# Scoring two groups and summing two pieces in one visit of TensorE, in a fused attention and squared-ReLU MLP loop

## The chip, the cores and the metric

The kernel runs on one NeuronCore of a Trainium2 chip. The metric is the device time of one execution in microseconds (us). The engines are named as in the profile: PE (TensorE matmul), PEld (its weight loads), DVE (VectorE), ACT (ScalarE), POOL (GpSimd) and SP (SyncE, whose queue issues the DMAs). Each works through its own instructions strictly in the order in which they were written, and waits on semaphores for the others.

## The reference

```python
B, N, C = (4, 12480, 128); n_agents = 49; d_ff = 2048
scale = 1.0 / np.sqrt(q.shape[-1])
def sm(a, b):
    s = scale * (a @ b.transpose(0, 2, 1))
    s = s - s.max(-1, keepdims=True)
    e = np.exp(s)
    return e / (e.sum(-1, keepdims=True) + 1e-09)
agent_v = sm(agents, k) @ v
x = (sm(q, agents) @ agent_v).reshape(B * N, C)
h = x @ w_in
r = np.maximum(h, 0.0)
return (r * r) @ w_out
```

Per batch, 49 agents attend to 12480 keys and gather `agent_v`; then each of the 12480 queries attends to the 49 agents, and its result goes through an MLP of width 2048 with a squared ReLU. All is float32.

## The kernel before

**Tiling.** Tokens come in groups of 960 (8 chunks of 120): 13 groups per batch and 52 in all. Query groups are numbered s = 0 to 51, the pieces of keys and values n = 0 to 12 in their batch b. The attention output is never formed: `w_make` multiplies `agent_v` into `w_in` once per batch (`w_hi`, `w_lo`), and the loop multiplies the query probabilities (`p_a`, and `p_b`, the same with its two halves of partitions exchanged by two DMAs, `q_spread`) by that product.

**The main loop** has 832 steps i, 16 per query group. Step i does `mm1` on PE (six matmuls into a tile `h`; there are two `h` buffers), `relu` on ACT (`h` to `rg`), and at odd steps, for the two steps together, `square` on ACT, `high` on DVE (`gh`, a rounded copy of `rg`) and `low` on DVE (`gl`, the remainder). About five steps later `mm2` (twelve matmuls) multiplies `gh` and `gl` by `wo_hi` and `wo_lo` and adds into a pair of PSUM banks. There are two such pairs. Eight steps make one output tile of 480 tokens in one pair; then `store` empties it (ACT and DVE, then a DMA), and the pairs change places.

**Visits.** The attention work of later groups is woven into the loop. Its matmuls go on PE between two steps and write into the pair that `mm2` is not using (`bank()`); here this is called a visit. Before there are these visits, for each group or piece: `k_scores` (keys times agents, 16 float32 matmuls of 49 columns), `q_scores` (the same for queries), `q_transpose` and `v_acc` (16 matmuls of 258 columns). Each is followed by a reader of the bank: `k_copy` (ACT), `q_shift` (DVE: `q_max` and `q_sub`), `q_copy` (ACT) and `v_sum` (DVE, adds into `acc`). Behind `q_shift` come `q_exp` on ACT, `q_inverse` on DVE, `q_norm` on POOL, `q_hi` on ACT, `q_lo` on POOL, then `q_transpose`. For keys and values: `k_pmax` on DVE, later `k_sub` (POOL), `k_exp` and `k_hi` (ACT), `k_lo` (POOL), `v_hi` (ACT) and `v_lo` (DVE), then `v_acc`. Batch 0's keys and values are done ahead of the loop; those of batches 1, 2 and 3 during the groups of the batch before.

**What sets the order.** A planner, `chain`, puts each part at a step number t, and all parts are written out sorted by t. A visit stands at t = g + .45, and g must be a step in `slots`: three of the eight steps of an output tile. ACT and DVE get at most one such part per step (`taken`) at + .5. In a step: `mm1` at + 0, `relu` at + .1, `mm2` and `store` at + .2, `square` at + .55, `high` at + .6, `low` at + .65. A DVE part that reads a bank right behind a visit stands at + .47 of the visit's step, and the `low` of the pair of steps before is then set to + .48 (`read`), that is, behind it. Loads are put some steps ahead of their use (`k_load`, `q_load`, `v_load`); they share five buffers (tag `io`) in the order in which they are written, and SP issues all DMAs from one queue.

Of the kernel before, what the change touches and what calls it, by code (L numbers as in the profile page):

```python
# [9 lines left out]
F32 = mybir.dt.float32  # L10
# [15 lines left out]
def agent_attention_relu2_kernel(ctx: ExitStack, tc: tile.TileContext, qT, kT, v, agT, w_in, w_out, outT):  # L26
# [14 lines left out]
    A2 = 2 * A  # L41
# [3 lines left out]
    rc = (slice(0, L), slice(L, CH))  # L45
# [10 lines left out]
    ag_sb = cpool.tile([P, B, A], F32, name="ag_sb")  # L56
# [69 lines left out]
    sk = cpool.tile([CH, NCH, A], F32, name="sk")  # L126
    pm = cpool.tile([CH, NS, A], F32, name="pm")
# [10 lines left out]
    H = G // 2  # L138
    halves = (slice(0, H), slice(H, G))

    kts, vts, pes, pss, two = {}, {}, {}, {}, [None]
# [5 lines left out]
    def bank():  # L147
        if now[0] is None:
            return ps_h.tile([P, 2, 512], F32, name="h")
        return pairs[now[0]]  # L150
# [4 lines left out]
    def piece(n):  # L155
        return sk[:, n * G:(n + 1) * G, :]
# [2 lines left out]
        kts[b, n] = (wk if b + n // 4 == 0 else io).tile([P, G, CH], F32, name="kt", tag="io" if b + n // 4 else turned[n])  # L159
        nc.sync.dma_start(out=kts[b, n], in_=kT[b, n])  # L160

    def scores(ps, x, b, cs=range(G)):
        for c in cs:
            for r in rc:
                nc.tensor.matmul(ps[r, 0, c * A:(c + 1) * A], x[:, c, r], ag_sb[:, b, :], start=True, stop=True)  # L165
        return ps[:CH, 0, :G * A].rearrange("p (c a) -> p c a", a=A)

    def k_scores(b, n):
        pss["k", n] = scores(bank(), kts.pop((b, n)), b)

    def k_copy(n):
        nc.scalar.copy(piece(n), pss.pop(("k", n)))

    def k_pmax(n):
        nc.vector.tensor_reduce(out=pm[:, n, :], in_=piece(n).rearrange("p c a -> p a c"), axis=AX.X, op=ALU.max)

    def k_pmax_bank(n):
        nc.vector.tensor_reduce(out=pm[:, n, :], in_=pss["k", n].rearrange("p c a -> p a c"), axis=AX.X, op=ALU.max)  # L178

    def k_max(step):  # L180
        if step == 0:
# [37 lines left out]
    vss = []  # L219
# [10 lines left out]
        vs = vss[n % 2][:, halves[h]]  # L230
        eng.tensor_tensor(out=vs[:, :, C + 2:], in0=vts[n][:, halves[h], :C], in1=vs[:, :, :C].bitcast(F32), op=ALU.subtract)

    def v_acc(n):
        vs, pe = vss[n % 2], pes.pop(n)
        vts.pop(n)
        pss["v", n] = bank()
        for c in range(G):
            for u in range(2):
                nc.tensor.matmul(pss["v", n][:A2, u, :VW], pe[rc[u], c, :], vs[rc[u], c], start=c == 0, stop=c == G - 1)  # L239

    def v_acc_whole(n, ps):

# [50 lines left out]
        else:  # L293
            nc.vector.tensor_tensor(wl[:, js], pss.pop(("w", b, j)), wh[:, js].bitcast(F32), op=ALU.subtract)

    PT, qs, es, mxs, sms, pps = {}, {}, {}, {}, {}, {}

    def q_load(s):
        qs[s] = (io if s else wk).tile([P, G, CH], F32, name="qt", tag="io" if s else "p_b")
        nc.sync.dma_start(out=qs[s], in_=qT[s])  # L300

    def q_scores(s):
        pss["q", s] = scores(bank(), qs.pop(s), s // NS)

    def q_scores_part(s, x):
        if x == 0:
            pss["q", s] = bank()
            scores(pss["q", s], qs[s], s // NS, range(H))
        else:
            pss["q", s] = scores(pss["q", s], qs.pop(s), s // NS, range(H, G))  # L310

    def q_max(s):
        mxs[s] = wk.tile([CH, G, 1], F32, name="mx")
        nc.vector.tensor_reduce(out=mxs[s], in_=pss["q", s], axis=AX.X, op=ALU.max)

    def q_sub(s):
        es[s] = wk.tile([CH, G, A], F32, name="e")
        nc.vector.tensor_tensor(es[s], pss.pop(("q", s)), mxs.pop(s).to_broadcast([CH, G, A]), op=ALU.subtract)

    def q_shift(s):  # L320
        q_max(s)
        q_sub(s)

    def q_exp(s):
        nc.scalar.activation(es[s], es[s], AF.Exp, scale=scale)
# [94 lines left out]


    LAG = 5
    AHEAD = 0
    steps = []

    def at(t, f, *args):
        steps.append((t, len(steps), f, args))
# [3 lines left out]
    hop = {"PE": {"PE": 1, "ACT": 1, "DVE": 0}, "ACT": {"PE": 2, "ACT": 1, "DVE": 0, "POOL": 0, "SP": 0},  # L431
           "DVE": {"PE": 2, "ACT": 1, "DVE": 1, "POOL": 1, "SP": 0}, "POOL": {"PE": 3, "ACT": 2, "DVE": 2, "POOL": 1}}
# [6 lines left out]
    def chain(t, todo):  # L439

        first = prev = None
        while todo:
            n = 1
            while todo[0][0] == "PE" and n < len(todo) and todo[n][1] in reads_bank and todo[n][0] != "PE":
                n += 1
            t += hop[prev][todo[0][0]] if prev else 0
            while True:
                g, p, ts = t, None, []  # L450
                for e, *_ in todo[:n]:
                    g += hop[p][e] if p else 0
                    while (e, g) in taken or (e == "PE" and g not in slots):
                        if p == "PE" and e == "DVE":
                            break
                        g += 1
                    ts.append(g)
                    p = e
                if todo[0][0] != "PE" or ts[-1] <= ts[0] + 1:
                    break  # L460
                t += 1
            for (e, f, *args), g in zip(todo, ts):
                soon = e == "DVE" and prev == "PE"
                if soon:
                    read.add(g)
                else:
                    taken.add((e, g))
                at(g + (.47 if soon else .45 if e == "PE" else .5), f, *args)
                prev = e
            first = ts[0] if first is None else first  # L470
            t, todo = ts[-1], todo[n:]
        return first, t

    reads_bank = (k_copy, k_max, v_sum, a_final, w_make, q_shift, q_copy)

    def plan_tokens(s, base):
        todo = [("PE", q_scores, s), ("DVE", q_shift, s), ("ACT", q_exp, s), ("DVE", q_inverse, s),
                ("POOL", q_norm, s), ("ACT", q_hi, s), ("POOL", q_lo, s),
                ("PE", q_transpose, s), ("ACT", q_copy, s)]
        first, end = chain(base, todo if s > 1 else todo[2:])  # L480
        if s > 1:
            at(first - 6, q_load, s)
        at(end + .9, q_spread, s)
        assert end + 3 < s * NF, (s, end)

    def plan_batch(b, base):

        end = b * NS * NF
        for n in range(NS):
            if b == 1 and n < AHEAD:  # L490
                continue
            first, t = chain(base + int(n * 4.6), [("PE", k_scores, b, n), ("ACT", k_copy, n), ("DVE", k_pmax, n)])
            if b > 1 or n:
                at(max(base - (6 if b > 1 else 0), first - 8), k_load, b, n)
            if n == NS - 2:
                chain(t + 1, [("DVE", k_max, 0)])
        _, t0 = chain(t + 1, [("DVE", k_max, 1), ("PE", k_max, 2), ("DVE", k_max, 3), ("PE", k_max, 4), ("DVE", k_max, 5)])
        free = {}
        d = (end - 37 - t0) / NS
        for n in range(NS):  # L500
            t, r = t0 + 1 + int(n * d), free.get(n - 2, 0) + 1
            first, _ = chain(max(t - 2, r), [("ACT", v_hi, n, 0), ("DVE", v_lo, n, 0)])
            _, t2 = chain(max(t - 1, r), [("ACT", v_hi, n, 1), ("DVE", v_lo, n, 1)])
            at(first - 6, v_load, b, n)
            _, t1 = chain(max(t, r - 3), [("POOL", k_sub, n), ("ACT", k_exp, n), ("ACT", k_hi, n), ("POOL", k_lo, n)])
            _, t = chain(max(t1 + 3, t2 + 2), [("PE", v_acc, n), ("DVE", v_sum, n)])
            free[n] = t - 1
        _, e = chain(t + 1, [("DVE", a_final, 0, b), ("PE", a_final, 1, b), ("DVE", a_final, 2, b)])
        for j in range(0, NJ, 4):
            _, e = chain(e + 2, [("PE", w_make, b, j // 4, j, 4, 0), ("ACT", w_make, b, j // 4, j, 4, 1), ("DVE", w_make, b, j // 4, j, 4, 2)])  # L510
        assert e + 2 < end, (e, end)
        return t + 1
# [28 lines left out]
    for n in range(NS):  # L541
        t = Z + 6.3 + 2.07 * n
        at(t, use, None if n % 3 else 1)
        at(t, k_scores, 0, n)
        at(t + .1, warm_up, 5 if n < NS - 1 else 0)
        at(t + 1.5, k_pmax_bank, n)
        at(t + 1.51, k_copy, n)
# [8 lines left out]
    at(t0 - 1.1, k_max, 0)  # L556
    at(t0 - .24, use, None)
    at(t0 - .23, q_scores_part, 0, 0)
    at(t0 - .1, use, 1)
    at(t0 - .05, warm_up, 2)  # L560
    for x, y in zip(range(1, 6), (-.1, 0, .5, .6, 2.6)):
        at(t0 + y, k_max, x)
    at(t0 + .3, warm_up, 2)
    at(t0 + .65, q_scores_part, 0, 1)
    at(t0 + .66, warm_up, 2)
    t0 += 2
# [18 lines left out]
    t = t0 + 15.9  # L585
# [72 lines left out]
```

## Time and profile before

| | |
|---|---|
| median of 3 runs | 1908.52 us (1907.07 to 1908.65) |
| the profiled execution | 1906.95 us |
| its span, first to last instruction | 1905.2 us |
| TensorE clock granted | 0.999 |
| PE busy | 1892.5 us (99%) |
| DVE busy | 1750.9 us (92%) |
| ACT busy | 1721.8 us (90%) |
| POOL busy | 355.3 us (19%) |

A group's row in the profile has the line, the engine, the operation, the tiles written and read, the count, the busy time, the mean duration of one in ns, and the idle time of the engine before it with what ended it. Records of one instruction overlap by about a tenth of a microsecond with the next on ACT and DVE, so the pitch is shorter than the duration. A row of the timeline has start and duration in us. The first step of the loop starts at 55.4 us.

### The profile page before, as it was taken

Reading aid. Unit: us, or ns where it says so; the run is one execution under the profiler, and the core shown is the slowest. Engines: PE = TensorE matmul, PEld = TensorE weight load, DVE = VectorE, ACT = ScalarE, POOL = GpSimd, SP = SyncE. Lnnn points to the kernel's source line nnn. Section 1 sums busy time; section 2 is a strip of 40 time slices with the busy share of each in tenths; the row PEclk is TensorE's granted clock in tenths of the full one; section 3 lists DMA queues with packets and bytes.
Section 4 is the critical chain, followed back from the end, with each engine's and each line's share of the span. In section 5 each row is a group of like instructions: output and inputs, shape, how many; then the busy total and the mean of one; then the engine's idle time right before and its main releaser. Section 6 shows DMA issues by size and latency. Waiting matters only on the chain.

```text
span 1905.2 us, 45852 instructions
## 1 busy us (share of the span) xinstructions
PE 1892.5 (99%) x20204; PEld 1669.1 (88%) x20204; DVE 1750.9 (92%) x1476; ACT 1721.8 (90%) x1809; POOL 355.3 (19%) x199
## 2 busy tenths in 40 slices
PE   9999999999999999999999999999999999999998
PEld 8788889988888998898888898998988888888888
DVE  7888999999889999999888999999989898989987
ACT  5788999998888999999888999999989999999997
POOL 0110233231012223324001223224201010000100
PEclk9999999999999999999999999999999999999999
DMA  9322222311331221211232121221211111111110
GB/s 369 107 71 82 83 63 62 92 42 51 104 98 41 81 63 53 75 57 57 79 97 62 57 75 52 66 79 41 64 36 35 50 33 53 36 36 53 35 38 22
DMA packets 44760, 130.95 MB, mean 69 GB/s; under 512 B 5034, under 2 KB 18474, under 8 KB 44562
## 3 DMA queue, kind: packets, MB, share of 16 engines
q1 hardware_dynamic: 44562, 128.04, 21.7%
q8 instruction: 158, 2.59, 0.6%
q14 instruction: 40, 0.33, 0.1%
HBM read 82.89 MB, written 25.56 MB: 57 GB/s over the span
## 4 chain that ended last, share of the span: by engine, by line
PE 96%; DVE 2%; DMA 1%; ACT 1%; issue 0%; SPq 0%; DVEq 0%
PE pair L412 57%; PE h L384 29%; PE pair L165 5%; PE pair L239 2%; PE pair L352 2%; DMA raw<-w_in 1%; DVE gl L401 0%; PE pair L290 0%; DMA kt<-kT 0%; DMA vt<-v 0%; DVE sk L197 0%; ACT rg L393 0%; DVE pm L178 0%; DVE cv L100 0%; DVE gh L397 0%; DVE cv L101 0%
## 5 line engine op out<-in xcount | busy, mean ns | idle before, releaser
L401 DVE TENSOR_TENSOR gl<-rg,gh 128x1920 fp32r<-128x1920 f32 x416 | 947.9, 2279 | 14.9 <-DVE gh L397 0.9
L390 ACT ACTIVATE rg<-h 128x960 f32<-128x960 f32 x832 | 804.5, 974 | 139.7 <-PE h L384 139.1
L393 ACT ACTIVATE rg<-rg 128x1920 f32<-128x1920 f32 x416 | 756.4, 1818 | 5.9
L412 PE MATMUL pair<-gh,wo_lo 64*128 64x480 f32 x3328 | 655.8, 378 | 0.0
L412 PE MATMUL pair<-gh,wo_hi 64*128 64x480 f32 x3328 | 654.7, 378 | 0.4 <-DVE gh L397 0.4
L397 DVE CAST gh<-rg 128x1920 fp32r<-128x1920 f32 x416 | 503.3, 1210 | 95.7 <-ACT rg L393 88.6
L384 PE MATMUL h<-p_a,w_hi 49*128 49x480 f32 x1664 | 511.8, 386 | 0.6 <-ACT rg L390 0.6
L412 PE MATMUL pair<-gl,wo_hi 64*128 64x480 f32 x3328 | 509.7, 376 | 1.8 <-DVE gl L401 1.8
L384 PE MATMUL h<-p_b,w_hi 49*128 49x480 f32 x1664 | 507.6, 385 | 0.0
L412 PEld LDWEIGHTS pair<-gh,wo_lo 64*128 64x128 f32 x3328 | 339.1, 186 | 36.3
L412 PEld LDWEIGHTS pair<-gh,wo_hi 64*128 64x128 f32 x3328 | 336.5, 184 | 37.6 <-DVE gh L397 0.8
L412 PEld LDWEIGHTS pair<-gl,wo_hi 64*128 64x128 f32 x3328 | 329.7, 184 | 44.0 <-DVE gl L401 4.2
L384 PEld LDWEIGHTS h<-p_a,w_hi 49*128 49x128 f32 x1664 | 291.1, 185 | 27.2 <-issue 2.4
L384 PE MATMUL h<-p_a,w_lo 49*128 49x480 f32 x832 | 311.1, 374 | 0.0
L384 PE MATMUL h<-p_b,w_lo 49*128 49x480 f32 x832 | 311.1, 374 | 0.0
L384 PEld LDWEIGHTS h<-p_b,w_hi 49*128 49x128 f32 x1664 | 293.1, 185 | 13.6
L337 POOL TENSOR_TENSOR e<-e,sm 120x392 f32<-120x392 f32 x51 | 80.7, 1582 | 1023.5 <-DVE sm L334 865.7
L384 PEld LDWEIGHTS h<-p_a,w_lo 49*128 49x128 f32 x832 | 152.6, 183 | 17.9
L384 PEld LDWEIGHTS h<-p_b,w_lo 49*128 49x128 f32 x832 | 152.7, 184 | 0.7
L344 POOL TENSOR_TENSOR pp<-e,pp 120x392 fp32r<-120x392 f32 x51 | 96.8, 1898 | 150.3 <-ACT pp L341 150.3
L207 POOL TENSOR_TENSOR pe<-sk,pe 120x392 fp32r<-120x392 f32 x39 | 76.5, 1962 | 253.3 <-ACT pe L204 253.3
L197 POOL TENSOR_TENSOR sk<-sk,mM 120x392 f32<-120x392 f32 x39 | 97.0, 2488 | 0.0
(112 smaller groups left out, 1170.9 us busy)
## 6 DMA issues: line engine op xcount, KB each, us to landing
vt<-v SPq DMA_DIRECT2D x52, 516.0 KB
kt<-kT SPq DMA_DIRECT2D x52, 480.0 KB
qt<-qT SPq DMA_DIRECT2D x52, 480.0 KB
outT<-ob SPq DMA_DIRECT2D x104, 240.0 KB
p_b<-p_a SPq DMA_DIRECT2D x104, 183.8 KB
raw<-w_in SPq DMA_DIRECT2D x4, 512.0 KB
raw<-w_out SPq DMA_DIRECT2D x4, 512.0 KB
ag_sb<-agT SPq DMA_DIRECT2D x1, 98.0 KB
```

What stands on the lines that cost most here:

```text
L165: nc.tensor.matmul(ps[r, 0, c * A:(c + 1) * A], x[:, c, r], ag_sb[:, b, :], start=True, stop=True)
L197: eng.tensor_tensor(out=piece(n), in0=piece(n), in1=m.rearrange("p (o a) -> p o a", o=1).to_broadcast([CH, G, A]), op=ALU.subtract)
L207: eng.tensor_tensor(out=pes[n][:, :, A:], in0=piece(n), in1=pes[n][:, :, :A].bitcast(F32), op=ALU.subtract)
L239: nc.tensor.matmul(pss["v", n][:A2, u, :VW], pe[rc[u], c, :], vs[rc[u], c], start=c == 0, stop=c == G - 1)
L337: eng.tensor_tensor(out=es[s], in0=es[s], in1=sms.pop(s).to_broadcast([CH, G, A]), op=ALU.mult)
L344: eng.tensor_tensor(out=pps[s][:, :, L:], in0=es.pop(s), in1=pps[s][:, :, :A].bitcast(F32), op=ALU.subtract)
L384: nc.tensor.matmul(h[:, u, :TT], w[ra[u], j, :], PT[s][u ^ lo][ra[u], cs, :], start=x == 0, stop=x == 2)
L390: nc.scalar.activation(rgs[p][:, x], hs.pop(i)[:, :, :TT], AF.Relu)
L393: nc.scalar.activation(rgs[p], rgs[p], AF.Square)
L397: nc.vector.tensor_copy(ghs[p], rgs[p])
L401: nc.vector.tensor_tensor(out=gls[p], in0=rgs.pop(p), in1=ghs[p].bitcast(F32), op=ALU.subtract)
L412: nc.tensor.matmul(outs[t][u][:, :TT], w[rg[u], 2 * j + e, :], g[rg[u], e, :], start=j == 0 and x == 0, stop=j == NJ - 1 and x == 5)
```

## The change

Scores of two groups go into the two banks of one pair in one visit, and one instruction reads both: `k_copy` for two key pieces, the two instructions of `q_shift` for query groups s and s + 1 (s even, from 2). `v_acc` accumulates two pieces in one visit, and `v_sum` adds them together. All other parts remain one for each group or piece. `k_copy` moves from the step behind the visit to the visit's own step, at + .47 (`ACTs`). `q_shift` moves from + .47 to + .49, behind `low`; `v_sum` stays at + .47. The exponentials, sums and transposes of the odd groups come some 15 steps behind those of the even ones. The two buffers of the shifted scores become one tile `eb`. Two loads of a pair are written at the same place.

```diff
-    def k_scores(b, n):
-        pss["k", n] = scores(bank(), kts.pop((b, n)), b)
-
-    def k_copy(n):
-        nc.scalar.copy(piece(n), pss.pop(("k", n)))
+    def both(ps, n):
+        return ps[:CH, :n, :G * A].rearrange("p u (c a) -> p u c a", a=A)
+
+    def k_scores(b, n, m=1):
+        ps = bank()
+        for u in range(m):
+            scores(ps, kts.pop((b, n + u)), b, u)
+        pss["k", n] = both(ps, m)
+
+    def k_copy(n, m=1):
+        nc.scalar.copy(sk[:, n * G:(n + m) * G, :].rearrange("p (u c) a -> p u c a", u=m), pss.pop(("k", n)))
...
+    def v_acc(n, m):
+        ps = pss["v", n] = bank()
+        for x in range(n, n + m):
+            vs, pe = vss[x % 2], pes.pop(x)
+            vts.pop(x)
+            for c in range(G):
+                for u in range(2):
+                    nc.tensor.matmul(ps[:A2, u, :VW], pe[rc[u], c, :], vs[rc[u], c], start=x == n and c == 0, stop=x == n + m - 1 and c == G - 1)
...
-    def q_scores(s):
-        pss["q", s] = scores(bank(), qs.pop(s), s // NS)
+    def q_scores(s, m=1):
+        ps = bank()
+        for u in range(m):
+            scores(ps, qs.pop(s + u), (s + u) // NS, u)
+        pss["q", s] = both(ps, m)
...
+    def q_shift(s, m=1):
+        mx = wk.tile([CH, 2, G, 1], F32, name="mx")[:, :m]
+        for x in range(s, s + m):
+            es[x] = eb[:, x % 2]
+        nc.vector.tensor_reduce(out=mx.rearrange("p u c o -> p u (c o)"), in_=pss["q", s], axis=AX.X, op=ALU.max)
+        nc.vector.tensor_tensor(eb[:, s % 2:s % 2 + m], pss.pop(("q", s)), mx.to_broadcast([CH, m, G, A]), op=ALU.subtract)
...
-                soon = e == "DVE" and prev == "PE"
-                if soon:
+                soon = e in ("DVE", "ACTs") and prev == "PE"
+                if soon and e == "ACTs":
+                    e = "ACT"
+                elif soon:
                     read.add(g)
                 else:
                     taken.add((e, g))
-                at(g + (.47 if soon else .45 if e == "PE" else .5), f, *args)
+                at(g + (.49 if soon and f is q_shift else .47 if soon else .45 if e == "PE" else .5), f, *args)
...
-        first, end = chain(base, todo if s > 1 else todo[2:])
-        if s > 1:
-            at(first - 6, q_load, s)
+        if s > 1 and s % 2 == 0:
+            first, base = chain(base, [("PE", q_scores, s, 2), ("DVE", q_shift, s, 2)])
+            for x in (s, s + 1):
+                at(first - 6, q_load, x)
+            base += 1
+        _, end = chain(base, todo)
...
+        for n in range(0, NS, 2):
+            m = min(2, NS - n)
+            first, t = chain(base + int(n * 4.6), [("PE", k_scores, b, n, m), ("ACTs", k_copy, n, m)])
+            for x in range(n, n + m):
+                _, t = chain(t + 1, [("DVE", k_pmax, x)])
+                if b > 1 or x:
+                    at(max(base - (6 if b > 1 else 0), first - 8), k_load, b, x)
...
+            if n % 2 or n == NS - 1:
+                x = n - n % 2
+                _, t = chain(max(done[y] for y in range(x, n + 1)), [("PE", v_acc, x, n + 1 - x), ("DVE", v_sum, x)])
+                for y in range(x, n + 1):
+                    free[y] = t - 1
```

Three places show how it moves the instructions. The first is DVE around the last query visit of the run: `gl` is `low`, `gh` is `high`, `mx` and the subtraction into `e` are `q_shift`, the three `sm` rows are `q_inverse`. Before:

```order
L397 CAST gh<-rg 128x1920
L314 TENSOR_REDUCE mx<-pair_103 120x8
L318 TENSOR_TENSOR e<-pair_103,mx 120x392
L401 TENSOR_TENSOR gl<-rg,gh 128x1920
L329 TENSOR_REDUCE sm<-e 120x8
```

Now:

```order
L403 CAST gh<-rg 128x1920
L407 TENSOR_TENSOR gl<-rg,gh 128x1920
L327 TENSOR_REDUCE mx<-pair_104 120x16
L328 TENSOR_TENSOR e<-pair_104,mx 120x784
L335 TENSOR_REDUCE sm<-e 120x8
```

The two readers of the bank have moved behind `gl` and are twice as wide.

The second is ACT around the same visit, where the order is the same before and now: the exponential of `e` stands between the two `rg<-h` (`relu`) of the visit's pair of steps and `rg<-rg` (`square`).

```order
L396 ACTIVATE rg<-h 128x960 x2
L331 ACTIVATE e<-e 120x392
L399 ACTIVATE rg<-rg 128x1920
L396 ACTIVATE rg<-h 128x960 x2
L399 ACTIVATE rg<-rg 128x1920
```

Nothing moved here, but the exponential's input is now written by an instruction that comes later on DVE.

The third is SP at the start of the loop: the first rows are written ahead of step 0, the last `p_b` rows are the two transfers for query group 1 (`q_spread`), `kt` and `qt` are loads of keys and queries, `outT` is a store. Before:

```order
L361 DMA p_b<-p_a 49x960 x2
L368 DMA held<-p_b 1x1
L160 DMA kt<-kT 128x960
L300 DMA qt<-qT 128x960
L160 DMA kt<-kT 128x960 x2
L361 DMA p_b<-p_a 49x960 x2
L419 DMA outT<-ob 128x480
```

Now:

```order
L367 DMA p_b<-p_a 49x960 x2
L374 DMA held<-p_b 1x1
L161 DMA kt<-kT 128x960 x2
L307 DMA qt<-qT 128x960 x2
L161 DMA kt<-kT 128x960 x4
L367 DMA p_b<-p_a 49x960 x2
L425 DMA outT<-ob 128x480 x2
```

Four more loads stand between `held` and `p_b`: eight instead of four. The last of the eight waits for PE, because it takes the buffer from which the visit of step 14 reads query group 2.

More of the change, by code (lines that the diff above doesn't have):

```diff
@@ L64, in agent_attention_relu2_kernel @@
     ppb = [cpool.tile([CH, G, AW], F32R, name=f"pp{x}") for x in range(2)]
+    eb = cpool.tile([CH, 2, G, A], F32, name="e")
     for x in ppb:
@@ L160, in k_load, with scores @@
         nc.sync.dma_start(out=kts[b, n], in_=kT[b, n])
-    def scores(ps, x, b, cs=range(G)):
+    def scores(ps, x, b, u=0, cs=range(G)):
         for c in cs:
             for r in rc:
-                nc.tensor.matmul(ps[r, 0, c * A:(c + 1) * A], x[:, c, r], ag_sb[:, b, :], start=True, stop=True)
-        return ps[:CH, 0, :G * A].rearrange("p (c a) -> p c a", a=A)
-    def k_scores(b, n):
-        pss["k", n] = scores(bank(), kts.pop((b, n)), b)
-    def k_copy(n):
-        nc.scalar.copy(piece(n), pss.pop(("k", n)))
+                nc.tensor.matmul(ps[r, u, c * A:(c + 1) * A], x[:, c, r], ag_sb[:, b, :], start=True, stop=True)
+    def both(ps, n):
[7 more added lines that the diff above has]
+        nc.scalar.copy(sk[:, n * G:(n + m) * G, :].rearrange("p (u c) a -> p u c a", u=m), pss.pop(("k", n)))
     def k_pmax(n):
@@ L177, in k_pmax_bank @@
     def k_pmax_bank(n):
-        nc.vector.tensor_reduce(out=pm[:, n, :], in_=pss["k", n].rearrange("p c a -> p a c"), axis=AX.X, op=ALU.max)
+        nc.vector.tensor_reduce(out=pm[:, n, :], in_=pss["k", n][:, 0].rearrange("p c a -> p a c"), axis=AX.X, op=ALU.max)
     def k_max(step):
@@ L231, in v_lo @@
         eng.tensor_tensor(out=vs[:, :, C + 2:], in0=vts[n][:, halves[h], :C], in1=vs[:, :, :C].bitcast(F32), op=ALU.subtract)
[L233 to L239, printed above, removed]
+    def v_acc(n, m):
[6 more added lines that the diff above has]
+                    nc.tensor.matmul(ps[:A2, u, :VW], pe[rc[u], c, :], vs[rc[u], c], start=x == n and c == 0, stop=x == n + m - 1 and c == G - 1)
     def v_acc_whole(n, ps):
@@ L294, in w_make @@
             nc.vector.tensor_tensor(wl[:, js], pss.pop(("w", b, j)), wh[:, js].bitcast(F32), op=ALU.subtract)
-    PT, qs, es, mxs, sms, pps = {}, {}, {}, {}, {}, {}
+    PT, qs, es, sms, pps = {}, {}, {}, {}, {}
     def q_load(s):
@@ L307, in q_scores_part @@
             pss["q", s] = bank()
-            scores(pss["q", s], qs[s], s // NS, range(H))
+            scores(pss["q", s], qs[s], s // NS, 0, range(H))
         else:
[L310 to L322, printed above, removed]
+            scores(pss["q", s], qs.pop(s), s // NS, 0, range(H, G))
+            pss["q", s] = both(pss["q", s], 1)
+    def q_shift(s, m=1):
[4 more added lines that the diff above has]
+        nc.vector.tensor_tensor(eb[:, s % 2:s % 2 + m], pss.pop(("q", s)), mx.to_broadcast([CH, m, G, A]), op=ALU.subtract)
     def q_exp(s):
@@ L422, in agent_attention_relu2_kernel @@
     LAG = 5
-    AHEAD = 0
     steps = []
@@ L451, in chain @@
                 for e, *_ in todo[:n]:
-                    g += hop[p][e] if p else 0
+                    g += (0 if p == 'PE' and e == 'ACTs' else hop[p][e]) if p else 0
                     while (e, g) in taken or (e == "PE" and g not in slots):
-                        if p == "PE" and e == "DVE":
+                        if p == "PE" and e in ("DVE", "ACTs"):
                             break
@@ L476, in plan_tokens @@
     def plan_tokens(s, base):
-        todo = [("PE", q_scores, s), ("DVE", q_shift, s), ("ACT", q_exp, s), ("DVE", q_inverse, s),
-                ("POOL", q_norm, s), ("ACT", q_hi, s), ("POOL", q_lo, s),
+        todo = [("ACT", q_exp, s), ("DVE", q_inverse, s), ("POOL", q_norm, s), ("ACT", q_hi, s), ("POOL", q_lo, s),
                 ("PE", q_transpose, s), ("ACT", q_copy, s)]
-        first, end = chain(base, todo if s > 1 else todo[2:])
-        if s > 1:
-            at(first - 6, q_load, s)
+        if s > 1 and s % 2 == 0:
[4 more added lines that the diff above has]
+        _, end = chain(base, todo)
         at(end + .9, q_spread, s)
@@ L488, in plan_batch @@
         end = b * NS * NF
[L489 to L495, printed above, removed]
+        for n in range(0, NS, 2):
[5 more added lines that the diff above has]
+                    at(max(base - (6 if b > 1 else 0), first - 8), k_load, b, x)
+            if n == NS - 3:
                 chain(t + 1, [("DVE", k_max, 0)])
         _, t0 = chain(t + 1, [("DVE", k_max, 1), ("PE", k_max, 2), ("DVE", k_max, 3), ("PE", k_max, 4), ("DVE", k_max, 5)])
-        free = {}
+        free, done = {}, {}
         d = (end - 37 - t0) / NS
@@ L505, in plan_batch @@
             _, t1 = chain(max(t, r - 3), [("POOL", k_sub, n), ("ACT", k_exp, n), ("ACT", k_hi, n), ("POOL", k_lo, n)])
-            _, t = chain(max(t1 + 3, t2 + 2), [("PE", v_acc, n), ("DVE", v_sum, n)])
-            free[n] = t - 1
+            done[n] = max(t1 + 3, t2 + 2)
+            if n % 2 or n == NS - 1:
[3 more added lines that the diff above has]
+                    free[y] = t - 1
         _, e = chain(t + 1, [("DVE", a_final, 0, b), ("PE", a_final, 1, b), ("DVE", a_final, 2, b)])
```

## Prediction, made before the changed kernel was run

> **What bounds the kernel now.** I read the page first (busy shares and the chain that ended last), then the groups of instructions, then short stretches of the timeline, where one step follows the next.
>
> ```profile
> span 1905.2 us, 45852 instructions
> PE 1892.5 (99%) x20204; PEld 1669.1 (88%) x20204; DVE 1750.9 (92%) x1476; ACT 1721.8 (90%) x1809; POOL 355.3 (19%) x199
> PE 96%; DVE 2%; DMA 1%; ACT 1%; issue 0%; SPq 0%; DVEq 0%
> PE pair L412 57%; PE h L384 29%; PE pair L165 5%; PE pair L239 2%; PE pair L352 2%; DMA raw<-w_in 1%; DVE gl L401 0%; PE pair L290 0%; DMA kt<-kT 0%; DMA vt<-v 0%; DVE sk L197 0%; ACT rg L393 0%; DVE pm L178 0%; DVE cv L100 0%; DVE gh L397 0%; DVE cv L101 0%
> ...
> L384 PE MATMUL h<-p_a,w_hi 49*128 49x480 f32 x1664 | 511.8, 386 | 0.6 <-ACT rg L390 0.6
> L412 PE MATMUL pair<-gl,wo_hi 64*128 64x480 f32 x3328 | 509.7, 376 | 1.8 <-DVE gl L401 1.8
> ```
>
> TensorE is the bound: 96% of the chain is PE, and it waited 0.6 us for ScalarE's `rg` and 1.8 us for VectorE's `gl` in the whole run. So a microsecond of PE time saved in the loop is a microsecond of span, as long as no feeder becomes late. ACT at 90% and DVE at 92% are not far off, which is where the danger lies. L165 (scores) is 5% of the chain and L239 (values) 2%; these are the visits that the change merges. One score visit near the end of the run, with its neighbours on all engines:
>
> ```profile
> 1757.49 0.38 PE L384 MATMUL h<-p_a,w_hi 49*128 49x480 f32 x1
> ...
> 1759.40 1.16 DVE L397 CAST gh<-rg 128x1920 fp32r<-128x1920 f32 x1
> 1759.56 1.01 PEld L165 LDWEIGHTS pair<-ag_sb,qt 128*64 128x64 f32 x32 [0.34 <-DVE gl L401]
> 1759.56 1.13 PE L165 MATMUL pair<-ag_sb,qt 128*64 128x49 f32 x32
> 1760.63 0.48 PE L384 MATMUL h<-p_a,w_hi 49*128 49x480 f32 x1
> 1760.75 0.57 DVE L314 TENSOR_REDUCE mx<-pair 120x8 f32<-120x392 f32 x1 [0.19 <-PE pair L165]
> ...
> 1761.42 0.57 DVE L318 TENSOR_TENSOR e<-pair,mx 120x392 f32<-120x392 f32 x1
> 1761.59 0.97 ACT L390 ACTIVATE rg<-h 128x960 f32<-128x960 f32 x1 [1.37 <-PE h L384]
> 1761.90 2.15 DVE L401 TENSOR_TENSOR gl<-rg,gh 128x1920 fp32r<-128x1920 f32 x1
> 1762.45 0.52 ACT L325 ACTIVATE e<-e 120x392 f32<-120x392 f32 x1
> 1762.70 0.38 PE L384 MATMUL h<-p_a,w_hi 49*128 49x480 f32 x1
> 1762.88 1.80 ACT L393 ACTIVATE rg<-rg 128x1920 f32<-128x1920 f32 x1
> ...
> 1764.57 1.91 ACT L390 ACTIVATE rg<-h 128x960 f32<-128x960 f32 x2
> 1764.66 0.38 PE L384 MATMUL h<-p_a,w_hi 49*128 49x480 f32 x1
> ...
> 1766.62 0.38 PE L384 MATMUL h<-p_a,w_hi 49*128 49x480 f32 x1
> ```
>
> The L384 rows at 1757.49, 1760.63, 1762.70, 1764.66 and 1766.62 start five successive steps g to g+4. A step without a visit takes 1.96. The step with the visit takes 3.14, and the one behind it 2.07: the visit costs 1.18 + 0.11 = 1.29. Its 32 weight loads of about 0.14 each fill 1.01, so sixteen pairs of loads follow each other every (1.01 - 0.14) / 15 = 0.058 and one group is worth 16 x 0.058 = 0.93. The other 0.36 is entering and leaving: the loads stood idle for 0.34 before the visit, and the next step's first matmul takes 0.48 instead of 0.38.
>
> **The change, part by part.** *Scores.* Thirteen key pieces in each of three batches become seven visits, so 18 visits go; query groups 2 to 51 go from 50 visits to 25. That is 43 entries and exits: 43 x 0.36 = 15.5 off PE. From the matmul row instead (1.13 less 0.22 for the last, over 15) the step is 0.061, one group 0.97 and the fixed part 0.32: 13.8. I take 15.0. The matmuls themselves stay.
>
> *Values.* Here 39 visits become 21:
>
> ```profile
> 422.15 0.38 PE L384 MATMUL h<-p_a,w_hi 49*128 49x480 f32 x1
> ...
> 424.11 1.13 PE L239 MATMUL pair<-vs,pe 64*98 64x258 f32 x16
> 425.08 0.39 PE L384 MATMUL h<-p_a,w_hi 49*128 49x480 f32 x1
> ...
> 427.04 0.38 PE L384 MATMUL h<-p_a,w_hi 49*128 49x480 f32 x1
> ```
>
> The step with the visit takes 2.93, the next 1.96: cost 0.97. Sixteen matmuls of 0.28 in 1.13 are eight pairs every 0.121, which is 0.97. The fixed part is nothing, and 18 visits fewer save at most 0.2 on PE.
>
> *Readers.* 18 `v_sum`, 18 `k_copy` and 25 times the two instructions of `q_shift` go, and the rest get wider. DVE's slope from 0.57 at 392 elements to 2.15 at 1920 is 1.03 ns per element, so each half of a double `q_shift` takes 0.57 + 0.41 = 0.98. VectorE is relieved by some 20 in all and ScalarE by 2 or 3, but neither ends the chain, so I book nothing. `k_copy` now stands on ACT directly behind the first `relu` and waits there for PE's visit. In the stretch above ACT stood idle 1.37 at this place, until the next step's `h`; the copy of about 0.82 fits between the end of the visit and that `h` (1759.56 + 1.13 = 1760.69 to 1761.59). Nothing booked; without this cover it would be 0.8 for each of 18.
>
> *`q_shift` behind `low`.* This is the first loss. VectorE now does `gh`, `gl`, then `mx` and `e` over 784, and the exponential that stands on ACT between `relu` and `square` of step g+1 waits for `e`. On the times above: `gh` ends at 1760.56, `gl` runs to 1762.75, `mx` to 1763.65, and `e`, a tenth later, to 1764.73. The exponential starts at 1764.76 instead of 1762.45. ACT is strict order: `square`, 0.43 later (1762.45 to 1762.88), starts at 1765.19, and the `relu` of step g+2, 1.69 behind (1762.88 to 1764.57), at 1766.88, ending at 1767.85. There are two `h` buffers, so mm1 of step g+4 needs that `relu`. Its old start is 1766.62, and with the longer visit 1767.55. It comes 0.35 late, allowing 0.05 for the signal. Where another visit stands two steps behind (11 of the 25 query visits by the order), PE is itself later by more than that, and nothing is lost. 14 places remain: 14 x 0.35 = 4.9. The price grows with the end of `gh`, which is here 3.07 behind the step's start, but elsewhere later:
>
> ```profile
> 707.40 0.38 PE L384 MATMUL h<-p_a,w_hi 49*128 49x480 f32 x1
> ...
> 710.19 1.16 DVE L397 CAST gh<-rg 128x1920 fp32r<-128x1920 f32 x1
> ```
>
> That one ends 3.95 behind, and would cost 1.23. Six of the 14 places lie after the last batch, where the first stretch holds; for the other eight I add a third of the difference, 8 x 0.3 = 2.4. Behind four of these the order has two or three more ACT instructions before the next visit. ACT needs 2 x 0.86 (1761.59 to 1762.45) + 1.69 = 3.41 for two steps and PE 3.92, so only 0.51 is free for them and each such place loses about 0.35 more: 1.4. The holds cost 8.7 in all, between 0 (if ACT catches up unseen) and 14 x 1.23 = 17.
>
> *DMA queue.* This is the second loss, and it happens once. SP's order puts loads of key pieces 4 and 5 of batch 1 ahead of the two `p_b` transfers of query group 1. The load of piece 5 takes the buffer of query group 2, which is read in the visit of step 14. Before, `p_b` was issued five steps ahead of step 16, which needs it.
>
> ```profile
> 48.91 1.64 SPq L361 DMA_DIRECT2D p_b<-p_a  x2
> 53.19 0.62 SPq L368 DMA_DIRECT2D held<-p_b  x1
> 55.44 0.69 PE L384 MATMUL h<-p_b,w_hi 49*128 49x480 f32 x2
> 80.44 1.55 SPq L361 DMA_DIRECT2D p_b<-p_a  x2
> 84.26 0.58 SPq L160 DMA_DIRECT2D kt<-kT  x1
> 87.14 1.13 PE L165 MATMUL pair<-ag_sb,qt 128*64 128x49 f32 x32
> 90.29 0.38 PE L384 MATMUL h<-p_a,w_hi 49*128 49x480 f32 x1
> 30.00:40.00 10.00, 8.28 (x129) 6.77 (x125) 8.51 (x19) 5.59 (x12) 1.42 (x3) 0.83 1.02 407
> PE pair L187 <- ACT sk L172: 1.7, 1, 1.7
> ```
>
> On the old clock the first group's matmuls end at 88.27. Then SP issues the load (0.6), and `p_b` starts at about 88.9. How long it takes is bounded by the first `p_b`: its first half was in when `held` read it, 53.19 - 48.91 = 4.3, and the whole of it when step 0 used it, 55.44 - 48.91 = 6.5. Step 16, at 90.29 + 0.93 = 91.2, would then start at 93.2 to 95.4, 2.0 to 4.2 late. Both halves are needed and a 480 KB load goes ahead, so I take 4.0.
>
> An idle PE also loses its clock: the stretch 30 to 40 us (the row before the last: PE busy 8.28, granted clock 0.83), with a PE wait of 1.7 in it (last row, of the waits between 28 and 40 us), was short of full clock by 0.17, so 10 x 0.17 = 1.7 was lost. I add 1.7 for the stall at step 16. The Trainium skill ("TensorE: Matmul & The Clock Gate", Part 1: The HAM clock gate) says that the clock halves after at least one idle window of about 3.4 us. By that rule alone a stall of 2.0 would cost no clock, and the whole sum would be 1903.3 with the short stall, and 1907 with mine; this trace shows the half clock after a shorter wait, and so I follow the trace.
>
> At the start, batch 1's first visit moves from step 7 to step 5 and `k_copy` delays a `square` there: half a microsecond either way, booked at 0.
>
> *Sum.* The profiled execution took 1906.95 (1905.2 span and 1.75 around it), 0.08% under the median 1908.52 of the runs. 1906.95 - 15.0 - 0.2 + 8.7 + 4.0 + 1.7 = 1906.2. With up to 1 for a `gl` or a bank that comes late once or twice: 1907.
>
> **Rivals.** *Faster: the losses don't reach PE.* For it: PE's waits for ACT are 0.6 now, and ACT has 139 us of idle time in front of `relu`:
>
> ```profile
> ACT rg L390 <- PE h L384: 139.1, 161, 1.5
> ```
>
> Against it: that idle lies just at the visits, and the exponential's wait takes it away at its own visit. Without the `p_b` stall the time is 1907 - 5.7 = 1901, without the holds 1898, without both 1892.6.
>
> *Slower: ACT becomes the bound between visits.* In the value phase most stretches of eight steps now have at most a transpose visit. ACT has some six extra instructions of 0.43 to 0.51 there, about 2.8, against 4 x 0.51 = 2.0 free. The margin is that `relu` of step g+2 ended by 1765.54 and its `h` was wanted at 1766.62, about 1.1. If ACT enters such a stretch already more than 0.3 behind, it comes through late. Some twenty such stretches at 0.5 are 10: 1917. Against it: a `gl` that does not wait for `q_shift` and 20 us less DVE work.
>
> *The gain is not there:* if the second group pays entry and exit again, because it goes to the other bank, the 15 stay and the time is 1922. The steady pitch inside a visit, across eight chunks, speaks against it.
>
> **How the numbers follow.** This measurement can tell about 0.2%, 3.8 us, from no change. My forecast, gain and losses about cancelling, within 0.2%, has 0.44. The faster rival has 0.35 in its three forms, ACT as the bound 0.17, and the missing gain 0.04, so slower has 0.21. The range reaches down to 1897 (the holds half and no `p_b` stall: 1907 - 4.4 - 5.7) and up to 1914 (the holds at 16 instead of 8.7); 1892.6, 1917 and 1922 stay outside with 2 in 10.
>
> **What the profile after would show.** L165's loads still sum to the same time, but in 64s; steps with a double visit take about 1.96 + 2.1. PE waits on `rg` rise from 0.6 to several us, in single waits of 0.3 to 1.3 four steps behind query visits, with ACT idle before L325's successor on DVE `e`. In step 16 PE waits once for some 4 us on `p_b`, near 91 us, and the clock of the next stretch is below 1. The `gl` waits stay near 2. If PE's waits on `rg` stay under 2 us, the holds are wrong; if no wait on `p_b` shows, the DMA step is; if many short waits on `rg` lie far from query visits, it is the ACT rival.

## The result, and the profile after

| | before | changed |
|---|---|---|
| median | 1908.40 us (1907.07 to 1908.65, 4 runs) | 1929.36 us (1928.50 to 1932.59, 4 runs) |
| ratio | | 1.0114, 95% interval 1.0097 to 1.0132 |
| profiled execution | 1906.95 us, span 1905.2 | 1928.50 us, span 1926.4 |

The change costs 21 us, or 1.1%. The forecast was no change, in a range that ended at 1914. First the page of the changed kernel:

```profile
span 1926.4 us, 45774 instructions
PE 1892.4 (98%) x20204; PEld 1665.4 (86%) x20204; DVE 1739.2 (90%) x1408; ACT 1722.2 (89%) x1791; POOL 349.2 (18%) x199
PE 61%; DVE 18%; ACT 14%; issue 5%; DMA 1%; SPq 0%; DVEq 0%; ACTq 0%
```

DVE's busy time, in which overlaps of records count once, fell by 12 us (the rows of `q_shift` and `v_sum` by 20, as the prediction has it), and still the span grew. The chain tells why: PE had 96% of it and now has 61%, and a third lies on DVE and ACT. PE's busy time is the same to 0.1 us, though 15 us of entries and exits are gone: busy records also cover part of the waiting (a step that comes 0.34 late below shows 0.17 of idle PE), so it says nothing here. The waits, of PE's weight loads and of ACT, say more. First three rows of before, then the same waits and two new ones after:

```profile
PEld pair L412 <- DVE gl L401: 4.2, 7, 1.5
PEld h L384 <- ACT rg L390: 2.2, 3, 1.0
ACT e L325 <- DVE e L318: 1.3, 1, 1.3
```

```profile
ACT e L331 <- DVE e L328: 47.3, 26, 3.5
PEld h L390 <- ACT rg L396: 28.3, 43, 2.8
PEld pair L418 <- DVE gl L407: 15.9, 29, 1.5
PEld h L390 <- DMA p_b<-p_a: 3.1, 1, 3.1
PE pair L246 <- DVE e L328: 1.7, 2, 0.8
```

The columns are the total, the count and the longest in us. ACT stands 47 us in front of the exponential, and PE's loads wait 28 us for `relu` and 16 us for `gl`.

**A ledger by steps.** For each of the 831 step intervals I took the time from the first mm1 matmul to that of the next step, less 1.96, less the price of the visit in it and of the visit behind it (single score 1.29, double 2.21, single value 0.97, double 1.93, transpose 0.81, the small visits as in the trace of before). What is left is waiting. This is a sum worked out from the trace, and waits ended by the same cause are added up.

| | before | changed | difference |
|---|---|---|---|
| steps and visits without waits | 1834.0 | 1819.2 | -14.8 |
| mm1 of step g+4 waits, g the step of a double query visit (14 places) | 0 | 12.9 | +12.9 |
| next visit waits for the bank (3 steps) | 0 | 2.3 | +2.3 |
| step 16 on `p_b` | 0 | 3.2 | +3.2 |
| scattered late `gl` and `rg`, small waits, start of the loop | 1.8 | 18.2 | +16.4 |
| ahead of step 0 and behind the loop | 69.4 | 70.7 | +1.3 |

That is 21.3 in all, the difference of the spans before rounding. The last line varies between runs of kernels whose code there is the same (step 0 began at 55.3 to 56.9 us) and is not put down to the change.

One double visit near the end of the run, the counterpart of the stretch in the prediction:

```profile
1745.20 0.59 PE L390 MATMUL h<-p_a,w_hi 49*128 49x480 f32 x2
...
1747.10 1.16 DVE L403 CAST gh<-rg 128x1920 fp32r<-128x1920 f32 x1
1747.25 1.94 PEld L166 LDWEIGHTS pair<-ag_sb,qt 128*64 128x64 f32 x64 [0.34 <-DVE gl L407]
...
1748.29 2.16 DVE L407 TENSOR_TENSOR gl<-rg,gh 128x1920 fp32r<-128x1920 f32 x1
1749.25 0.48 PE L390 MATMUL h<-p_a,w_hi 49*128 49x480 f32 x1
...
1750.22 0.97 ACT L396 ACTIVATE rg<-h 128x960 f32<-128x960 f32 x1 [2.29 <-PE h L390]
1750.37 0.97 DVE L327 TENSOR_REDUCE mx<-pair 120x16 f32<-120x784 f32 x1
...
1751.44 0.97 DVE L328 TENSOR_TENSOR e<-pair,mx 120x784 f32<-120x784 f32 x1
...
1752.45 0.53 ACT L331 ACTIVATE e<-e 120x392 f32<-120x392 f32 x1 [1.26 <-DVE e L328]
1752.88 1.79 ACT L399 ACTIVATE rg<-rg 128x1920 f32<-128x1920 f32 x1
...
1755.59 0.48 PE L390 MATMUL h<-p_a,w_hi 49*128 49x480 f32 x1 [0.17 <-ACT rg L396]
```

The 64 loads take 1.94, against 1.01 for 32, with one idle stretch of 0.34 in front: the second group does come in for 0.93. The rest is the hold as forecast: `gh`, `gl`, `mx`, `e`, ACT idle for 1.26 with `square` and the next `relu` behind it in its queue, and mm1 of step g+4 late. Here the step comes out 0.34 late. In the value phase the same chain is longer:

```profile
387.35 1.15 DVE L403 CAST gh<-rg 128x1920 fp32r<-128x1920 f32 x1
...
388.54 2.80 DVE L407 TENSOR_TENSOR gl<-rg,gh 128x1920 fp32r<-128x1920 f32 x1
...
391.26 0.96 DVE L327 TENSOR_REDUCE mx<-pair 120x16 f32<-120x784 f32 x1
...
392.33 0.97 DVE L328 TENSOR_TENSOR e<-pair,mx 120x784 f32<-120x784 f32 x1
393.34 0.53 ACT L331 ACTIVATE e<-e 120x392 f32<-120x392 f32 x1 [3.45 <-DVE e L328]
```

`gh` ends 4.62 behind the start of its step (383.88), `gl` takes 2.80 where 2.15 is usual, beside a POOL instruction for part of that time, and ACT stands for 3.45. Mm1 four steps on is 2.5 late.

### The profile page after: what moved, and what is told of

The parts are those of the page before. It is cut to its first block, busy times and chain, and to the rows that moved or that the text cites. A ratio compares the mean times of both kernels' runs of the same rounds, so it can differ in the third digit from the quotient of the medians.

```text
span 1926.4 us, 45774 instructions
## 1 busy us (share of the span) xinstructions
PE 1892.4 (98%) x20204; PEld 1665.4 (86%) x20204; DVE 1739.2 (90%) x1408; ACT 1722.2 (89%) x1791; POOL 349.2 (18%) x199
## 3 DMA queue, kind: packets, MB, share of 16 engines
q1 hardware_dynamic: 44562, 128.04, 21.3%
## 4 chain that ended last, share of the span: by engine, by line
PE 61%; DVE 18%; ACT 14%; issue 5%; DMA 1%; SPq 0%; DVEq 0%; ACTq 0%
PE pair L418 35%; PE h L390 19%; DVE gl L407 7%; ACT rg L399 6%; ACT rg L396 6%; DVE gh L403 5%; PE pair L166 3%; PE pair L246 2%; PE pair L358 2%; DVE vs L237 1%; DVE e L328 1%; DVE mx L327 1%; DVE ob L424 1%; DMA raw<-w_in 1%; ACT p_a L362 1%
## 5 line engine op out<-in xcount | busy, mean ns | idle before, releaser
L403 DVE CAST gh<-rg 128x1920 fp32r<-128x1920 f32 x416 | 512.9, 1233 | 115.0 <-ACT rg L399 110.1
L390 PE MATMUL h<-p_a,w_hi 49*128 49x480 f32 x1664 | 511.7, 385 | 11.7 <-ACT rg L396 11.5
L418 PEld LDWEIGHTS pair<-gl,wo_hi 64*128 64x128 f32 x3328 | 325.5, 184 | 53.9 <-DVE gl L407 15.9
L418 PEld LDWEIGHTS pair<-gh,wo_lo 64*128 64x128 f32 x3328 | 335.0, 186 | 35.6
L343 POOL TENSOR_TENSOR e<-e,sm 120x392 f32<-120x392 f32 x51 | 62.3, 1222 | 946.8 <-DVE sm L340 685.3
L390 PEld LDWEIGHTS h<-p_a,w_lo 49*128 49x128 f32 x832 | 152.6, 183 | 14.8
L213 POOL TENSOR_TENSOR pe<-sk,pe 120x392 fp32r<-120x392 f32 x39 | 88.2, 2262 | 284.9 <-ACT pe L210 260.0
```

The lines of the kernel that those rows point to most:

```text
L213: eng.tensor_tensor(out=pes[n][:, :, A:], in0=piece(n), in1=pes[n][:, :, :A].bitcast(F32), op=ALU.subtract)
L343: eng.tensor_tensor(out=es[s], in0=es[s], in1=sms.pop(s).to_broadcast([CH, G, A]), op=ALU.mult)
L390: nc.tensor.matmul(h[:, u, :TT], w[ra[u], j, :], PT[s][u ^ lo][ra[u], cs, :], start=x == 0, stop=x == 2)
L403: nc.vector.tensor_copy(ghs[p], rgs[p])
L418: nc.tensor.matmul(outs[t][u][:, :TT], w[rg[u], 2 * j + e, :], g[rg[u], e, :], start=j == 0 and x == 0, stop=j == NJ - 1 and x == 5)
```

## Experiments

Times are medians. The differences are against the kernel before, run beside it on the same chip: 1907.55 for e1 to e4, 1907.45 for e5 to e8, 1907.84 for e9 to e11.

**e1: `q_shift` back ahead of `low`.**

```diff
-                at(g + (.49 if soon and f is q_shift else .47 if soon else .45 if e == "PE" else .5), f, *args)
+                at(g + (.47 if soon else .45 if e == "PE" else .5), f, *args)
```

> The changed kernel with one number back: q_shift at + .47 of the visit's step, ahead of low, as before the change. Theory 1 (the wait of the exponential for q_shift is what makes mm1 wait three steps behind a double query visit, and the bank is handed on late): the 12.9 us of those waits and the 2.3 us of bank waits go, the late gl of the value phase stay, so about 1929 - 15 = 1914 us. Rival A (the late gl and rg in stretches without visits are the backlog of the same hold, carried on): nearly all 35 us of waits go, about 1897. Rival B (low, now behind the wider q_shift, is late itself): the gain is eaten by new waits on gl, 1922 or more.

Measured 1911.32, ratio 1.0018 (1.0009 to 1.0028): 3.8 slower than before, where the changed kernel was 21.0 slower. This one number is worth 17 us. In its profile the waits at the places behind query visits and for the bank are gone from the ledger (15.2 to 0.2), and ACT's standing in front of the exponential is a fifth:

```profile
ACT e L331 <- DVE e L328: 9.5, 26, 1.3
PEld h L390 <- ACT rg L396: 6.0, 17, 1.0
PEld pair L418 <- DVE gl L407: 17.0, 29, 1.5
```

The late `gl` stay, as theory 1 has it: the scattered waits fall only by about a fifth. Rival A falls. The profiled execution (1908.02) was the fastest of ten; eight of the others had a lower mean clock (0.997 to 0.999, against 1.0).

**e2: `q_shift` still behind `low`, but the exponential behind `square`, and `q_inverse`, which reads its result, behind `low`.**

```diff
-                at(g + (... else .45 if e == "PE" else .5), f, *args)
+                at(g + (... else .45 if e == "PE" else .58 if f is q_exp and args[0] > 1 and args[0] % 2 == 0 else .7 if f is q_inverse and args[0] > 1 and args[0] % 2 == 0 else .5), f, *args)
```

> The changed kernel, q_shift still behind low, but for the even groups the exponential stands behind square on ACT (+ .58 for + .5) and q_inverse behind high and low on DVE (+ .7). Theory 1 (ACT standing still for the exponential is the cost, not q_shift's place on DVE): the 12.9 us of mm1 waits three steps behind the query visits go, the 2.3 us of bank waits stay, about 1916 us. Rival B (VectorE's order is the cost): no better than 1926.

Measured 1917.64, ratio 1.0049 (1.0034 to 1.0064): 10.1 slower than before, so 10.9 of the 21.0 are gone. The ledger's waits behind query visits fall from 12.9 to 1.2, the bank waits stay at 2.3, and the other waits rise by some 2. So it is ACT's strict order that carries the delay to PE: taking the waiting exponential out of `square`'s way is enough to free these steps, with `q_shift` behind `low` as in the change.

**e3: values one piece at a time, scores in pairs.**

```diff
-            done[n] = max(t1 + 3, t2 + 2)
-            if n % 2 or n == NS - 1:
-                ...
+            _, t = chain(max(t1 + 3, t2 + 2), [("PE", v_acc, n, 1), ("DVE", v_sum, n)])
+            free[n] = t - 1
```

> The changed kernel with v_acc and v_sum for one piece at a time again, scores still in pairs. Theory 1 (pairing the values leaves stretches of ten and more steps without a visit in which ACT and DVE fall behind, and saves PE nothing): most of the 14 us of scattered waits on gl and rg go, about 1916 us, while the 15 us at the query visits stay. Rival C (the scattered waits come from the fewer score visits, not from the value visits): no change beyond 3 us, 1926 to 1930.

Measured 1925.87, ratio 1.0092 (1.0077 to 1.0107): 18.3 slower than before, only 2.7 less than the changed kernel, a difference within the intervals of the two. Theory 1's account of the scattered waits was wrong, and rival C has them right: in the ledger they stay within half a microsecond of the changed kernel's. Some fell, and new ones appeared (0.9 at 287 us, 1.0 at 364 us), most of the larger ones five to eight steps behind the place where an odd query group had its visit. But the waits behind query visits and for the bank, which theory 1 expected to stay, fell from 15.2 to 8.5. Most of that does not show in the time of the profiled execution, because it ran two stretches of 3.4 us at half clock, at 97 and at 397 us, where the changed kernel's had none; the two steps there took 3.8 longer than in the changed kernel (0.7 of it a longer wait on `p_b`). So 2.7 is no clean price of the value pairs.

**e4: the kernel before with key pairs alone.** The diff is the change's own `k_scores`, `k_copy` and loop over pairs of pieces, without the rest.

> The kernel before with the key pairs alone: k_scores and k_copy for two pieces (k_copy in the visit's own step), queries and values one at a time. Theory 1 (a merged score visit saves its entry and exit, 0.35 us, and key pairs have no hold behind them): 18 x 0.35 = 6.3 us less than before, about 1902 us, and no load ahead of p_b. Rival C (fewer visits alone make the feeders late): 1907 or more.

Measured 1901.29, ratio 0.9967 (0.9954 to 0.9979): 6.26 less, where 18 x 0.35 = 6.3 was expected. The price of an entry and exit is right, and in the key phases nothing takes it back.

**e5: the kernel before with query pairs alone.**

> The kernel before with the query pairs alone, q_shift at + .47 as before; keys and values one at a time. By the visits alone 25 x 0.35 = 8.7 us less than before, about 1899 us. Theory 2 (the scattered late gl come where the odd group's visit has been taken away while its exponential, sum and the value work stay, so that PE has no pause in which DVE and ACT catch up): late gl and rg worth 5 to 9 us in the value phases, 1904 to 1908 us. Rival D (that needs the value pairs as well): 1898 to 1900.

The kernel that ran kept `q_shift` at + .49, behind `low`, other than the expectation says, so it tests something else: the query part of the change as it was made. Measured 1925.42, ratio 1.0093 (1.0078 to 1.0108), 18.0 slower: the query pairs by themselves bring nearly the whole loss.

**e6: the kernel before with value pairs alone.**

> The kernel before with the value pairs alone. Theory 2: the pairing saves PE nothing (a value visit has no fixed part) and bunches the pauses, so 0 to 3 us slower than before, 1907 to 1911 us. Rival E (18 v_sum fewer on DVE help): 1 us or more faster, below 1906.

Measured 1914.15, ratio 1.0035 (1.0022 to 1.0048), 6.7 slower, more than theory 2 allowed. The ledger behind step 20 has 9.6 of waiting against 2.9 before, mostly `gl` late by 0.2 to 1.4 in the first step of an output tile. The pairing itself saves PE nothing, as forecast (the visits come to -0.1).

**e7: e1 with 12 filler visits.**

```diff
+    def filler():
+        ps = bank()
+        for c in range(G):
+            for r in rc:
+                nc.tensor.matmul(ps[r, 0, c * A:(c + 1) * A], ident[:, r], ag_sb[:, 0, :], start=True, stop=True)
...
+        if s in (7, 9, 11, 17, 19, 21, 23, 29, 31, 33, 35, 37):
+            chain(base, [("PE", filler)])
```

> As the run with q_shift ahead of low, and in addition 12 visits of 16 float32 matmuls (constants, results unused) at the steps of the value phases where the odd query groups had their visits. If PE were the bound there: 12 x 1.29 = 15.5 us more than that run, about 1926. Theory 2 (PE waits there for DVE and ACT anyway, so that the taken-out visits were free time): well under half of that, up to 1918, with the waits on gl in those stretches gone.

Measured 1919.11, ratio 1.0062 (1.0045 to 1.0079), 11.7 slower than before and 7.9 more than e1. The fillers put 15.3 of work on PE, and half of it cost nothing: the ledger's waits behind step 20 go from 15.7 to 7.8. The total is just above what theory 2 set as its bound. So PE did wait for its feeders in these stretches, but less than the whole length of the visit that was taken out.

**e8: pairs only where there is slack.** Key pairs, query pairs for s = 2, 12, 14, 26 and 38 to 50, `q_shift` ahead of `low`, single values, and the late load behind `p_b`:

```diff
+    DOUBLE = (2, 12, 14, 26, 38, 40, 42, 44, 46, 48, 50)
...
+        m = 2 if s - s % 2 in DOUBLE else 1
+        if s > 1 and s % m == 0:
+            first, base = chain(base, [("PE", q_scores, s, m), ("DVE", q_shift, s, m)])
...
-                    at(max(base - (6 if b > 1 else 0), first - 8), k_load, b, x)
+                    at(max(base - (6 if b > 1 else 0), first - 8) if (b, x) != (1, 5) else 10.95, k_load, b, x)
```

> Key pairs throughout, query pairs only for 11 even groups whose odd partner's old visit lies outside the value phases (2, 12, 14, 26 and 38 to 50), q_shift at + .47, values one at a time, and the load of key piece 5 of batch 1 written behind p_b. Theory 2: 29 merged visits, 29 x 0.35 = 10.1 us less than before and no new waits, about 1897.5 us. If the late gl come back with query pairs anywhere: 1900 or more.

Measured 1897.82, ratio 0.9952 (0.9937 to 0.9967): 9.6 less than before, with 10.1 expected. This version beats both. Its waits behind step 20 are 3.6 against 2.9 before, and PE has its chain back:

```profile
PE 93%; DVE 4%; ACT 2%; issue 0%; DVEq 0%
```

**e9: the kernel before with query pairs alone, `q_shift` ahead of `low`.**

> The kernel before with the query pairs alone and q_shift at + .47, ahead of low (the run e5 kept it at + .49, behind low). By the visits alone 25 x 0.35 = 8.7 us less than before, about 1899 us. Theory 2 (the odd group's visit was the pause in which ACT and DVE caught up in the value phases): late gl of some 0.6 us in each of 12 stretches take most of it back, 1904 to 1908 us. Rival D (all of e5's loss was q_shift's place): 1898 to 1901.

Measured 1909.91, ratio 1.0012 (1.0002 to 1.0021): 2.1 slower than before, though the visits alone save 8.7. So 10.8 came back, more than theory 2's 5 to 9, and rival D falls. Against e5 the place of `q_shift` is worth 15.9, near e1's 17. One of these stretches, at 350 us, from the timeline:

```profile
350.27 2.87 POOL L213 TENSOR_TENSOR pe<-sk,pe 120x392 fp32r<-120x392 f32 x1
...
352.24 1.91 DVE L403 CAST gh<-rg 128x1920 fp32r<-128x1920 f32 x1
...
354.26 2.82 DVE L407 TENSOR_TENSOR gl<-rg,gh 128x1920 fp32r<-128x1920 f32 x1
...
357.00 1.45 DVE L237 TENSOR_TENSOR vs<-vt,vs 120x512 fp32r<-120x512 f32 x1
...
360.04 2.14 DVE L407 TENSOR_TENSOR gl<-rg,gh 128x1920 fp32r<-128x1920 f32 x1
...
362.24 0.71 PE L418 MATMUL pair<-gl,wo_hi 64*128 64x480 f32 x4 [0.77 <-DVE gl L407]
```

DVE runs without a pause, its instructions stretched beside POOL's (`gh` 1.91 where 1.15 is usual, `vs` 1.45 where 0.68 is), until PE waits for `gl`. Such stretched instructions are there before the change too, and in like number over the run (42 `gh` above 1.3 us then, 40 here; 82 `gl` above 2.5 then, 91 here; each of them beside a POOL instruction). What is missing is the odd group's visit at step 126, in which PE left DVE time. But DVE is late ahead of that place already: the `gl` of steps 112 and 113, right behind the double visit, ends 1.2 us after the start of step 117, whose `mm2` reads it, and before the change it ended 0.2 ahead of that start; one pair earlier the difference was 0.8. So a delay is there beforehand, the wider `q_shift`, which stands ahead of this `low`, adds to it, and no visit makes it good; no run separates these parts. About a quarter of the waits (3.1 us, in steps 85, 277, 309, 373 and 469) stand seven steps behind a double visit, where no odd group had its place; there the wider `q_shift` is the nearer cause.

**e10: the change with one load behind `p_b`** (the last line of e8's diff alone).

> The changed kernel with one load written later: key piece 5 of batch 1 behind the two p_b transfers of query group 1. Theory 1: the wait of step 16 for p_b goes (3.2 us in the profile), and with it the half clock that can follow it (1.7 us in some executions): 3 to 5 us less, 1924.5 to 1926.5. Rival F (the p_b wait is cover for DVE and ACT, and comes back at the next visits): less than 1.5 us.

Measured 1926.73, ratio 1.0100 (1.0085 to 1.0115): 18.9 slower than before, 2.1 less than the changed kernel, and within the intervals of the two. The wait of step 16 is gone from the profile. In the profiled execution about the same was lost to the clock: two stretches at half clock elsewhere, behind the waits near 318 and 393 us, cost some 1.6 each, as the section on the hardware shows. Between theory and rival F this is too close to call by time; by the ledger the 3.2 do not return as waits.

**e11: all score pairs, `q_shift` ahead, single values, the load behind `p_b`.**

> As the run with pairs where there is slack (1897.8), but with all 25 query pairs, 14 more of them with the odd group's old visit in the value phases or beside them. By the visits alone 14 x 0.35 = 4.9 us less, 1893. Theory 2: late gl and rg in the 12 stretches cost more than that, 1899 to 1906.

Measured 1904.11, ratio 0.9982 (0.9972 to 0.9991): 5.9 (with the difference to before, -3.7 against -9.6) worse than e8 with 14 visits fewer. Those 14 would save 4.9 and cost 10.8. The waits behind step 20 are 14.6 against e8's 3.6, 11.0 more:

```profile
PEld pair L418 <- DVE gl L407: 17.1, 23, 1.5
```

## Why the prediction was wrong

**Right: the price of a visit.** 15.0 were booked for 43 entries and exits; the ledger has 14.8 for all visits, e4 gives 6.26 for 18, and values save nothing. The rival in which the second group pays again fell with the 64 loads in 1.94.

**Right in mechanism, mis-sized: the hold behind query visits.** Booked 8.7 at 14 places; it is 12.9 at 14 places, 0.34 at each of the last six as worked out, but 0.55 to 2.5 at the other eight. I took a third of the way to the latest `gh` of the old trace (3.95); the new trace has 4.62, because ACT and DVE already came late into this visit (the `square` two steps ahead of it ends 5.0 behind the start of its step, 4.1 before the change). e1 and e2 show the mechanism. With the bank waits, which I had counted among "up to 1", `q_shift`'s place costs 15 in the ledger and 17 by e1's time.

**Right in mechanism: the wait on `p_b`.** Booked 4.0, measured 3.2, in step 16:

```profile
90.74 0.33 SPq L161 DMA_DIRECT2D kt<-kT  x1
91.13 1.54 SPq L367 DMA_DIRECT2D p_b<-p_a  x2
...
96.70 0.48 PE L390 MATMUL h<-p_b,w_hi 49*128 49x480 f32 x2 [2.70 <-DMA p_b<-p_a]
```

The transfer took 5.6 from its first issue, between the bounds 4.3 and 6.5. The 1.7 for the clock was not lost in this execution; it was in those of e3 and e7, where this wait was 3.8. The holds and this stall together were booked at 14.4 and measured 16.1: the two misses partly cancel.

**The step that failed: "With up to 1 for a `gl` or a bank that comes late once or twice".** The late `gl` and the rest are 16.4, the bank 2.3, and the 16.4 alone move the forecast from about 1906 to beyond the range. I had taken each gain of PE time as time gained unless a named wait stood against it. In the value phases ACT and DVE were only a few per cent short of PE (of the 200 us from 300 to 500 before, DVE was busy for 190 and ACT for 186), and a visit was not only PE's cost but the pause in which they caught up. The rival "ACT becomes the bound between visits" came near to this, with a margin worked out, and had 0.17. Its 10 us were too few, and the engine that came late most was DVE, which I had put on the side of relief: away from query visits 18 steps wait on `gl`, 9.4 us, and 13 on `rg`, 2.8 us, where the prediction had the `gl` waits stay near 2 and took many short waits on `rg` as the rival's sign. e7 and e9 show that PE time there is worth less than its length: half of the filler cost nothing, and the query pairs alone lose 10.8 without any hold. Value pairs alone cost 6.7 (e6), and taking them out of the change gives back 2.7 (e3); the clock lost in e3's profiled execution is nearly the size of the difference, so whether the parts add up stays open. Counting 20 us less DVE work against this rival was wrong too: e6 has half the `v_sum`, and its PE waits more for `gl` than before.

Not settled: how the late `gl` divides between the missing visit, the wider `q_shift` and the instructions of DVE that are stretched beside POOL. No run took POOL's work away or split `q_shift` again.

## What to carry to other kernels

When the bound engine has neighbours at 90%, ask stage by stage where they catch up, and leave the bound engine's small visits there; merge visits only in stages where the neighbours have room (here key phases and the tail: 9.6 us gained, against 21 lost). A wider reader that is moved behind a long instruction delays whoever consumes its result, and on an in-order engine everything queued behind that consumer. Load order matters in the same way: a prefetch that waits for a buffer holds back the urgent transfer written behind it.

## What the runs showed of the hardware

The TensorE clock fell to half, for 3.4 us at a time, after PE stalls in some executions and not in others, for stalls of the same size. The changed kernel and e10 have the same wait near 318 us, and the next ten microseconds are granted differently, changed kernel first, then its clock row, then the two of e10:

```profile
PEld h L390 <- ACT rg L396: 2.3, 1, 2.3
318.00:328.00 10.00, 8.07 (x90) 6.93 (x88) 8.19 (x9) 8.25 (x9) 2.92 (x3) 1.00 0.01 2
```

```profile
PEld h L390 <- ACT rg L396: 2.3, 1, 2.3
318.00:328.00 10.00, 10.00 (x94) 9.04 (x94) 7.52 (x7) 7.53 (x8) 1.95 (x2) 0.83 0.01 2
```

The granted clock (third column from the end) is 1.00 in the one and 0.83 in the other, 1.7 us lost. So a stall of 2.3 us costs the clock in one execution and not in another. Behind the wait on `p_b` the outcomes go with the length: it was 3.1 in the changed kernel, which kept 1.00 (first row), and 3.8 in e3, which had 0.83 (second row).

```profile
92.00:102.00 10.00, 7.30 (x110) 5.98 (x108) 7.88 (x9) 5.17 (x6) 0.85 (x1) 1.00 0.31 110
92.00:102.00 10.00, 6.57 (x90) 5.10 (x86) 6.53 (x8) 3.51 (x4) 0.84 (x1) 0.83 0.21 77
```

The Trainium skill ("TensorE: Matmul & The Clock Gate", Part 1: The HAM clock gate) says that the window of about 3.4 us is free-running and not tied to the kernel, which agrees with the same stall having both outcomes; that the half clock comes after a whole idle window agrees with the two waits on `p_b`, and does not agree with the loss after a wait of 2.3.
